# Where three groups of reads are queued in a fused attention gradient kernel: q's first weights, output weights, transposing reads

## The chip, the cores and the metric

The kernel runs on one core of a Trainium2 chip. The metric is the device time of one execution in microseconds; here it is the median of the runs of the kernel before and, after the change, of the changed kernel's runs beside it. A core has five engines that run their own instruction streams in order: PE (matmul, with its weight loads shown apart as PEld), DVE, ACT and POOL (element-wise work), and SP, which here only issues DMAs. POOL and ACT issue DMAs too. All DMAs of the core share 16 DMA engines.

## The reference, cut to what matters

Two attention blocks over 2048 rows of 448 values, 16 heads of 28, forward and gradient, all in bfloat16. Block A is linear attention with the feature map `phi`; block B is softmax attention with one key and value head shared by all 16 query heads.

```
def A(x, wqkv, wo):
    q, k, v = split_heads(x @ wqkv)
    pq, pk = phi(q), phi(k)          # phi(t) = where(t > 0, t + 1, exp(t)) + 1e-6
    kv = einsum("bhsd,bhse->bhde", pk, v);  z = einsum("bhsd->bhd", pk)
    num = einsum("bhqd,bhde->bhqe", pq, kv)
    den = einsum("bhqd,bhd->bhq", pq, z)[..., None] + 1e-6
    return merge_heads(num / den) @ wo

def B(x, wq, wk, wv, wo):
    q = split_heads(x @ wq);  k = x @ wk;  v = x @ wv
    p = softmax(einsum("bhqd,bkd->bhqk", q, k) * 28 ** -0.5)
    return merge_heads(einsum("bhqk,bkd->bhqd", p, v)) @ wo

out, vjp = jax.vjp(lambda *a: concat([A(a[:3]), B(a[3:])], -1), A_x, A_wqkv, A_wo, B_x, B_wq, B_wk, B_wv, B_wo)
return (out, *vjp(grad_out))
```

## The kernel before

Three stages follow each other.

*Prologue (up to the first scores).* `load_xb` reads B's x in four chunks of 512 rows on SyncE; `wq_nat` gets q's weights on POOL's queue, the first four heads (`G0` columns) ahead of the rest, each with one read for 384 rows and one for the last 64; ACT's queue reads k's and v's weights. On PE, `xb_tr(k)` transposes a chunk (ACT evacuates one half at L723, DVE the other at L725). `wq_pads` (L747) copies q's weights into a layout of 32 columns a head; `wkv_pads` (L727 to L734) does that for k and v and replicates them. `q_first` projects the first four heads of chunk 0 and computes the norm of each q row on DVE (L761 to L797); `kv_nat`, `k_sq` and `kv_rep` project k and v, take the norms of k, and write k transposed four times over (`kT_rep`). The largest k norm (`kmax_bc`, L907) and the q norm give an upper bound of each score, which is put in as an extra column (`q_col`), so that the exponential needs no row maximum. Then POOL issues the reads of A's weights (L888, L889), the 16 reads of B's output weights `woB_pr` (L894, one for each head) and those of A's x (L896).

*Forward sweep (256 steps, L1232).* A step takes four heads, 512 query rows and 128 key rows: PE forms scores (`pe_s`, `s_ps`), ACT takes the exponential (`act_e`, L990, two instructions a step), SyncE writes the result to DRAM (`write_e`, L997, 512 KB a step), PE accumulates the output (`pe_o`, `oacc`). The tile `e` comes from a pool of 5 buffers, so a step's exponential waits until the write of five steps ago has landed. Between these, `block` takes pieces off lists by a budget: each piece has a cost, and a step adds `pace(s)` to the budget, 1.15 for the first 128 steps. The order is fixed when the program is built, in the order of the code; a DMA in a piece goes to its engine's queue at that place and waits there for its inputs, with everything behind it.

The first list, `later`, holds the rest of B's q work: `q_rest`, then `bigs` (`q_proj` for chunks 1 to 3, and `kv_rep` for v), each followed by its `smalls[n]`: transposes of q and weights, `pad_next`, and `woT_f`, which transposes the output weights. In `q_proj`, DVE copies the projection (L778), POOL squares it (L779), and two steps later DVE sums it (L782); after the fourth, `q_norm` follows. Then come the pieces of block A (`pieces_A`): projections with `phi`, `G_part`, the rounds `p3_nd` to `p3_dk` over 16 row tiles, which need grad_out transposed (`gaT`), gradients of weights (`gw_all`), and the rounds `p5_dp0` to `p5_gx`, which need x transposed again (`xT`). `chunk_T` (L156 to L159) makes such a transposed chunk of 512 rows and 512 columns with one transposing DMA on SyncE from SBUF to SBUF. `p3_nd(i)` asks for the next chunk of `gaT` at i % 4 == 3; its source `ga` is read by `ga_load` after the round of `gwo` in which the old one was last used. `xT2(0)` stands ahead of `gw_all(3)`, and `p5_dp0(i)` asks for the next chunk at i % 4 == 1. `load_gbT` (L1036) reads and transposes B's part of grad_out from DRAM, 128 columns at a time, and `load_quarter` and `load_e` (L1173, L1165) read back the written exponentials, transposed.

*Backward sweep (L1348) and weight gradients (L1381 on).* Not touched by the change.

Of the kernel before, what the change touches and what calls it, by code (L numbers as in the profile page):

```python
# [12 lines left out]
BF16 = mybir.dt.bfloat16  # L13
# [4 lines left out]
D = 448  # L18
P = 128
# [5 lines left out]
def kernel(  # L25
# [21 lines left out]
    nc = tc.nc  # L47
# [3 lines left out]
    NQC = S // 512  # L51
# [89 lines left out]
    def pieces_A(gen, pl, post, flush, pre_tiles, pk_d, early, swap_pools):  # L141
# [3 lines left out]
        def piece(cost, cap=None):  # L145
            def add(fn):
                out.append((cost, fn, cap))
                return fn
            return add

        V = {}
# [4 lines left out]
        def chunk_T(src, nm):  # L156
            t = chk.tile([P, 4, 4, P], BF16, name=nm, tag="chunk")
            nc.sync.dma_start_transpose(t[:].rearrange("p b c s -> p (b c) s"), src.rearrange("p b d -> p (b d)"))
            return t  # L159

        def xchunk(qc):
            return V["x"][:, qc * 4:(qc + 1) * 4, :]

# [149 lines left out]
            V["gq"] = Halves(halves, "gq_A")  # L313

        def p3_nd(i):
            if i % 4 == 3 and i // 4 < 3:
                V["gaT", i // 4 + 1] = chunk_T(V["ga", i // 4 + 1], "gaT")
            ps = gen([P, 512], "ps_nd")
            for g in range(4):
                mm(ps[:, g * P:(g + 1) * P], V["pq"][:, i, g * P:(g + 1) * P], V["kvz"][:, g, :])  # L320
            rden = awk.tile([P, H, 1], F32, name="rden_A", bufs=3)
            nc.vector.reciprocal(out=rden[:], in_=hv(ps[:, :])[:, :, 0:1])
            nc.vector.tensor_tensor(out=hv(V["onat"][:, i, :]), in0=hv(ps[:, :]),
                                    in1=rden[:].to_broadcast([P, H, 32]), op=ALU.mult)
            V["rden", i] = rden
# [169 lines left out]
        def gw(src, c, q, bi):  # L495
            if q == 0:
                V["acc"] = gen([P, 512], "gw_acc")
            acc = V["acc"]
            for st in range(2 * q, 2 * q + 2):
                mm(acc[:, :], V["x"][:, st, c * P:(c + 1) * P], V[src][:, st, :], start=(st == 0), stop=(st == NS - 1))  # L500
            if q == 7:
                out_gw(acc, c, bi)

        def gw_all(c):
            for q in range(8):
                piece(0.43, 1.3)(lambda c=c, q=q: gw("gq", c, q, 0))
                if q % 4 == 3:
                    piece(0.0)(lambda k=2 * c + q // 4: part_pk2(k))
# [8 lines left out]
            V["natq"] = load_wnat(0, "wqA2")  # L517

        gw_all(0)

        def xT2(qc):
            V["xT", qc] = chunk_T(xchunk(qc), "xaT2")

        def wT_pad(nm):
            nat = V.pop("natq" if nm == "q" else "natk")
# [16 lines left out]
        gw_all(2)  # L542
        for g in range(4):
            piece(0.25)(lambda g=g: wT_tr("k", g))
        piece(0.0)(lambda: xT2(0))
        gw_all(3)

        def p5_dp0(i):
            if i % 4 == 1 and i // 4 < 3:
                xT2(i // 4 + 1)  # L550
            ps = gen([P, 512], "ps_dpk")
            for c in range(2):
                mm(ps[:, :], V["xT", i // 4][:, i % 4, c, :], V["Wp"][:, c, :], start=(c == 0), stop=False)
            V["dpk"] = ps
# [132 lines left out]
    def load_xb(k):  # L687
        nc.sync.dma_start(xb_n[k][:], Bx2[k * 512:(k + 1) * 512, :].rearrange("(b p) d -> p b d", p=P))

    for k in range(NQC):  # L690
        load_xb(k)
    G0 = 4 * DH
    wq_nat = w4.tile([P, 4, D], BF16, name="wqB_nat", tag="w4")
    nc.gpsimd.memset(wq_nat[0:64, 3, :], 0.0)
    for lo, hi in ((0, G0), (G0, D)):
        nc.gpsimd.dma_start(wq_nat[:, 0:3, lo:hi], B_wq[0:384, lo:hi].rearrange("(c p) f -> p c f", p=P))
        nc.gpsimd.dma_start(wq_nat[64:128, 3, lo:hi], B_wq[384:448, lo:hi])
    wkv_nat = tmp.tile([P, 4, 2 * DH], BF16, name="wkv_nat")
    nc.gpsimd.memset(wkv_nat[0:64, 3, :], 0.0)
    for i, w in enumerate((B_wk, B_wv)):  # L700
# [15 lines left out]
    def xb_tr(k):  # L716
        for c2 in range(2):
            tp = gen([P, 1024], "xbT_ps", BF16)
            for c in range(2):
                tr4(tp, lambda b: xb_n[k][:, b, XOFF[2 * c2 + c]:XOFF[2 * c2 + c] + P], 4 * c)  # L720
            dst = xbT[k][:, 2 * c2:2 * c2 + 2, :].rearrange("p c s -> p (c s)")
            if c2 == 0:
                nc.scalar.copy(out=dst, in_=tp[:, :])  # L723
            else:
                nc.vector.tensor_copy(out=dst, in_=tp[:, :])  # L725
# [20 lines left out]
    def wq_pads(h0, h1):  # L746
        nc.vector.tensor_copy(  # L747
            out=wq_pad[:].rearrange("p c (h x) -> p c h x", x=32)[:, :, h0:h1, 1:1 + DH],
            in_=wq_nat[:].rearrange("p c (h e) -> p c h e", e=DH)[:, :, h0:h1])

    def q_first():
        qn_t[0] = ptmp.tile([P, 4, 512], BF16, name="qn", bufs=3)
        nrm_t[0] = ptmp.tile([P, 4, H], F32, name="nrm2")
        pq = gen([P, 4, P], "projN_ps")
        for b in range(4):
            for dc in range(4):
                mm(pq[:, b, :], xbc(dc, b * P, P), wq_pad[:, dc, 0:P], start=(dc == 0), stop=(dc == 3))
        nc.scalar.copy(out=qn_t[0][:, :, 0:P], in_=pq[:, :, :])
        qsq = ptmp.tile([P, H, 32], F32, name="qsq")
        qv = qn_t[0][:].rearrange("p b (h c) -> p b h c", c=32)[:, :, 0:4, :]  # L760
        nc.vector.tensor_tensor(out=qsq[:].rearrange("p (b h) c -> p b h c", b=4), in0=qv, in1=qv, op=ALU.mult)  # L761
        nc.vector.tensor_reduce(out=nrm_t[0][:, :, 0:4], in_=qsq[:].rearrange("p (b h) c -> p b h c", b=4),
                                axis=AX.X, op=ALU.add)
        return upper_sqrt(ptmp, nrm_t[0][:, :, 0:4], [P, 4, 4], 0.5, "root4")
# [97 lines left out]
    def k_sq(hf):  # L862
# [2 lines left out]
        nc.vector.tensor_tensor(out=ksq[:, a], in0=kn[:, a, :], in1=kn[:, a, :], op=ALU.mult)  # L865
        nc.vector.tensor_reduce(out=kn2[:, a], in_=ksq[:, a], axis=AX.X, op=ALU.add)

    wq_pads(0, 4)
    xb_tr(0)
    rootq0 = q_first()  # L870
    wkv_pads()
    xb_tr(1)
    kv_nat(0)
    kv_nat(1)
    xb_tr(2)
    k_sq(0)
    kv_nat(2)
    kv_rep(0, 0, True)
    xb_tr(3)
    kv_nat(3)  # L880
    k_sq(1)
    for hf in range(2):
# [3 lines left out]
    for off in (D, 0, 2 * D):  # L886
# [1 line left out]
        nc.gpsimd.dma_start(nat[:, 0:3, :], A_wqkv[0:384, off:off + D].rearrange("(c p) f -> p c f", p=P))  # L888
        nc.gpsimd.dma_start(nat[0:64, 3, :], A_wqkv[384:448, off:off + D])  # L889
        nats.append(nat)  # L890
    for g in range(4):
        for j in range(4):
            h = 4 * g + j
            nc.gpsimd.dma_start(woB_pr[g][32 * j + 1:32 * j + 1 + DH, :], B_wo[h * DH:(h + 1) * DH, :])  # L894
    for k in range(2):
        nc.gpsimd.dma_start(x_nat.h[k][:, :, 0:D],  # L896
                            Ax2[k * S // 2:(k + 1) * S // 2, :].rearrange("(t p) d -> p t d", p=P))
# [2 lines left out]
    rootk = upper_sqrt(tmp, kcol[:], [P, 1], 0.5, "rootk")  # L900
    kdiag = tmp.tile([P, P], F32, name="kdiag")
    nc.vector.tensor_scalar(out=kdiag[:], in0=identF[:], scalar1=rootk[:, 0:1], scalar2=None, op0=ALU.mult)
    for b in range(1, 4):
        kv_rep(0, b, True)
    kbc_ps = gen([P, P], "kbc_ps")
    nc.tensor.matmul(kbc_ps[:, :], lhsT=onesF[:, :], rhs=kdiag[:, :], start=True, stop=True)
# [22 lines left out]
    for n in range(4):  # L929
        smalls[n + 4].append((0.3, lambda g=n: wqT(g)))  # L930
    smalls[5].append((0.25, wkvT))
    for n in (6, 9, 12):
        smalls[n].append((0.0, pad_next))
    for n, ci in ((7, 0), (10, 1), (14, 2), (15, 3)):
        smalls[n].append((0.25, lambda ci=ci: woT_f(ci)))
    for g in range(4):
        smalls[8 + g // 2].append((0.25, lambda g=g: q_tr(1, g)))
# [544 lines left out]
```

## Time and profile before

| | |
|---|---|
| time, median of 3 runs | 1329.32 us (1326.28 to 1336.55) |
| the profiled execution: time | 1330.31 us |
| the profiled execution: span | 1328.2 us, mean granted clock 0.971 |
| first score on PE | 29.40 us |
| forward sweep (first to last exponential) | 29.9 to 634.7 us |
| backward sweep | 638 to 1273 us |
| busy share of the span: PE, DVE, ACT, POOL | 93%, 71%, 80%, 19% |
| DMA: moved, mean rate | 321.76 MB, 242 GB/s |

Lines of the trace give the start and the length of an instruction or a run of equal ones in us, the engine, the line of the code, the operation, what it writes and reads, and how many; in brackets stands the idle time of the engine just before it and what ended it. SPq is SyncE's queue of DMA issues: the length there is the time of issuing, not of the transfer. Lines of waits give the sum in us, the number and the longest. A granted clock of 0.50 means that PE runs at half speed. The DMA share is the time that packets took, over 16 engines; it can pass 1.

### The profile page before, as it was taken

How to read it: one execution, taken by the hardware profiler on the slowest of the kernel's cores; microseconds unless marked ns; L12 is line 12 of the kernel's file. 1: busy time of each engine (PE TensorE's matmuls, PEld its weight loads, DVE VectorE, ACT ScalarE, POOL GpSimd, SP SyncE). 2: the span in 40 equal slices, each digit the busy share in tenths (PEclk: the TensorE clock that was granted, in tenths of full speed). 3: DMA queues.
4: the chain of work that ended last, by engine and by line, in shares of the span. 5: the costliest groups of instructions: out<-in, count | busy, mean ns of one | idle time of the engine just before them, and what ended most of it. 6: DMA issues, size and time to landing. Idle time of an engine off the chain costs nothing.

```text
span 1328.2 us, 30263 instructions
## 1 busy us (share of the span) xinstructions
PE 1233.2 (93%) x12630; PEld 595.0 (45%) x12690; DVE 940.1 (71%) x1211; ACT 1061.8 (80%) x1176; POOL 250.6 (19%) x317
## 2 busy tenths in 40 slices
PE   6878899888988998998899999999999999999998
PEld 4332234344422333332455555555555555555554
DVE  4775527677743334420789999999999999999942
ACT  3669998778877898996688888888888888888851
POOL 4510032333422112110013111111111111111110
PEclk7889999999989899998899999999999999999999
DMA  3766889589779989889999999999999999999832
GB/s 113 282 211 257 288 324 305 210 309 294 264 287 279 322 299 299 303 287 319 243 238 231 216 230 223 227 214 230 234 219 223 211 218 229 223 223 219 191 124 69
DMA packets 627193, 321.76 MB, mean 242 GB/s; under 512 B 572256, under 2 KB 587600, under 8 KB 626800
## 3 DMA queue, kind: packets, MB, share of 16 engines
q1 hardware_dynamic: 615984, 293.28, 86.6%
q0 software_dynamic: 9088, 26.45, 6.3%
q8 instruction: 99, 1.62, 0.6%
q10 hardware_dynamic: 1984, 0.10, 0.1%
q14 instruction: 38, 0.31, 0.1%
HBM read 23.71 MB, written 153.45 MB: 133 GB/s over the span
## 4 chain that ended last, share of the span: by engine, by line
PE 72%; issue 8%; ACT 7%; DVE 6%; POOL 3%; DMA 3%; SPq 1%; ACTq 0%; POOLq 0%; DVEq 0%
PE dsT_ps L89 19%; PE dp_ps L105 12%; PE akv L108 11%; PE s_ps L105 6%; PE dq_ps L108 5%; ACT e L990 4%; PE oacc L108 3%; DMA edram<-e 3%; PE ps_gx L85 2%; ACT phi_ex L168 2%; PE ps_gxB L85 1%; PE gwq_acc L85 1%; PE G_ps L85 1%; PE gwoB_ps L85 1%; PE ps_go L85 1%
## 5 line engine op out<-in xcount | busy, mean ns | idle before, releaser
L1279 DVE TENSOR_TENSOR ds<-dp_ps,eN 128x1024 bf16<-128x1024 f32 x512 | 604.8, 1220 | 25.5 <-PE dp_ps L105 13.0
L990 ACT ACTIVATE e<-s_ps 128x1024 bf16<-128x1024 f32 x512 | 499.6, 1077 | 105.3 <-issue 33.7
L1301 ACT ACTIVATE dsT<-dsT_ps 128x1024 bf16<-128x1024 bf16 x512 | 496.8, 1023 | 93.3 <-PE dsT_ps L89 93.1
L89 PE MATMUL dsT_ps<-identB,ds 128*128 128x128 bf16 x4096 | 274.8, 220 | 0.0
L89 PEld LDWEIGHTS <-ds 128*128 128x128 bf16 x4096 | 230.5, 98 | 59.3 <-issue 59.2
L105 PE MATMUL s_ps<-qT_B,kT_rep 32*128 32x512 bf16 x1024 | 185.5, 392 | 36.4 <-ACT e L990 30.2
L1331 POOL TENSOR_TENSOR dkv<-dkv,asb 128x512 f32<-128x512 f32 x60 | 76.1, 1268 | 494.1 <-ACT asb L1330 489.0
L108 PE MATMUL akv<-ds,qn_b 128*32 128x512 bf16 x1024 | 156.7, 386 | 0.0
L105 PE MATMUL dp_ps<-vT_rep,doT_b 32*128 32x512 bf16 x768 | 150.0, 387 | 3.5 <-DVE ds L1279 2.4
L105 PEld LDWEIGHTS <-kT_rep 32*128 32x128 bf16 x1024 | 53.6, 91 | 199.3 <-issue 190.6
L108 PE MATMUL akv<-eN,don_b 128*32 128x512 bf16 x768 | 117.7, 387 | 0.0
L108 PE MATMUL dq_ps<-dsT,kn 128*32 128x512 bf16 x1024 | 105.4, 379 | 0.2 <-ACT dsT L1301 0.2
L108 PE MATMUL oacc<-e,vaug 128*32 128x512 bf16 x1024 | 80.9, 393 | 0.0
L105 PEld LDWEIGHTS <-doT_b 32*128 32x128 bf16 x768 | 36.2, 91 | 95.8 <-issue 72.8
L108 PEld LDWEIGHTS <-kn 128*32 128x32 bf16 x1024 | 33.1, 97 | 39.9 <-issue 8.0
L105 PE MATMUL dp_ps<-vT_rep,doT_q 32*128 32x512 bf16 x256 | 49.6, 384 | 0.0
L596 DVE CAST gx_sb<-ps_gx 128x448 bf16<-128x448 f32 x16 | 10.0, 624 | 48.9 <-PE ps_gx L85 48.9
L108 PEld LDWEIGHTS <-don_b 128*32 128x32 bf16 x768 | 21.9, 94 | 43.9 <-issue 43.9
L169 DVE TENSOR_SCALAR phi_ex<-phi_ex 128x512 f32<-128x512 f32 x32 | 14.8, 462 | 34.2 <-ACT phi_ex L168 34.0
L108 PE MATMUL akv<-eN,don_q 128*32 128x512 bf16 x256 | 38.9, 384 | 0.0
L1330 ACT ACTIVATE asb<-akv 128x512 f32<-128x512 f32 x60 | 36.3, 605 | 0.0
L349 POOL TENSOR_SCALAR dph_A<-oq_A 128x512 bf16<-128x512 bf16 x16 | 30.6, 1912 | 29.9 <-issue 27.7
(286 smaller groups left out, 1226.5 us busy)
## 6 DMA issues: line engine op xcount, KB each, us to landing
edram<-e SPq DMA_DIRECT2D x256, 512.0 KB
eN<-edram SPq DMA_TRANSPOSE x137
pk_d<-pkn_A POOLq DMA_DIRECT2D x2, 1024.0 KB, 5.4
onat_d<-onat_q POOLq DMA_DIRECT2D x4, 512.0 KB, 6.3
pk_A<-pk_d POOLq DMA_DIRECT2D x8, 256.0 KB, 8.2
qn_b<-qn_d SPq DMA_DIRECT2D x16, 128.0 KB
on_nat<-onat_d SPq DMA_DIRECT2D x4, 512.0 KB
xb_nat<-in_B_x_dram SPq DMA_DIRECT2D x4, 448.0 KB
```

What stands on the lines that cost most here:

```text
L85: nc.tensor.matmul(out_ap, lhsT=lhsT, rhs=rhs, start=start, stop=stop, tile_position=(0, 0))
L89: nc.tensor.transpose(out_ps_ap, in_ap, ident[0:k, 0:k], tile_position=(0, 0))
L105: nc.tensor.matmul(out_ap, lhsT=lhsT, rhs=rhs, start=True, stop=True, tile_position=(32 * j, 0))
L108: nc.tensor.matmul(out_ap, lhsT=lhsT, rhs=rhs, start=start, stop=stop, tile_position=(0, 32 * c))
L168: nc.scalar.activation(out=ex[:], in_=ps[:, :], func=ACT.Exp)
L169: nc.vector.tensor_scalar(out=ex[:], in0=ex[:], scalar1=1.0, scalar2=1e-6, op0=ALU.min, op1=ALU.add)
L349: nc.gpsimd.tensor_scalar(out=dph[:], in0=oq[:, 512:1024], scalar1=-1e-6, scalar2=1.0, op0=ALU.add, op1=ALU.min)
L990: nc.scalar.activation(out=es[s][:].rearrange("p a j q -> p j a q")[:, 2 * hf:2 * hf + 2], in_=sps.pop(h)[:].rearrange("p j (a q) -> p j a ...
L1279: nc.vector.tensor_tensor(out=ds[:], in0=dps.pop(h)[:], in1=eNs[i][:, 2 * hf:2 * hf + 2, :], op=ALU.mult)
L1301: nc.scalar.activation(out=dsTs[kcu][:].rearrange("p t j q -> p j t q")[:, 2 * hf:2 * hf + 2, :, b * P:(b + 1) * P], in_=tps.pop(h)[:], fu ...
L1330: nc.scalar.activation(out=asb[:], in_=akv[:, :], func=ACT.Copy)
L1331: nc.gpsimd.tensor_tensor(out=dkv[:, kc * 512:(kc + 1) * 512], in0=dkv[:, kc * 512:(kc + 1) * 512], in1=asb[:], op=ALU.add)
```

## The change

q's first-group weights are read on SyncE behind chunk 0 of x and ahead of chunks 1 to 3; the second group stays on POOL. The copies `wq_pads` and `wkv_pads` stand behind the first evacuation, chunk 1's transposes go ahead of `q_first`, and the norm part of `q_first` becomes `q_first_norm`, behind `kv_nat(1)`. `kv_rep(0, 0)` joins the other three. The reads of `woB_pr` leave the end of the prologue for the slots 2 to 5 of the pieces, four in each, and the first `woT_f` moves from slot 7 to 8. `gaT` is made in two halves (at i % 4 == 2 and 3), and the later `xT` in four parts of 128 rows: those of chunk 0 among the pieces of `gw_all(3)`, those of the next chunk one in each round. In the built program SyncE issues 15 more transposes and 2 more reads.

```diff
+        def part_T(key, src, b0, b1):
+            if b0 == 0:
+                V[key] = chk.tile([P, 4, 4, P], BF16, name=key[0] + "_c", tag="chunk")
+            nc.sync.dma_start_transpose(V[key][:, b0:b1].rearrange("p b c s -> p (b c) s"),
+                                        src[:, b0:b1].rearrange("p b d -> p (b d)"))
...
         def p3_nd(i):
-            if i % 4 == 3 and i // 4 < 3:
-                V["gaT", i // 4 + 1] = chunk_T(V["ga", i // 4 + 1], "gaT")
+            if i % 4 >= 2 and i // 4 < 3:
+                b0 = 2 * (i % 4 - 2)
+                part_T(("gaT", i // 4 + 1), V["ga", i // 4 + 1], b0, b0 + 2)
...
+        def xT2(qc, b):
+            part_T(("xT", qc), xchunk(qc), b, b + 1)
+
         def gw_all(c):
             for q in range(8):
+                if c == 3 and q % 2 == 0:
+                    piece(0.0)(lambda b=q // 2: xT2(0, b))
...
-        def xT2(qc):
-            V["xT", qc] = chunk_T(xchunk(qc), "xaT2")
...
-        piece(0.0)(lambda: xT2(0))
         gw_all(3)
 
         def p5_dp0(i):
-            if i % 4 == 1 and i // 4 < 3:
-                xT2(i // 4 + 1)
+            if i // 4 < 3:
+                xT2(i // 4 + 1, i % 4)
...
-    for k in range(NQC):
-        load_xb(k)
...
-    for lo, hi in ((0, G0), (G0, D)):
-        nc.gpsimd.dma_start(wq_nat[:, 0:3, lo:hi], B_wq[0:384, lo:hi].rearrange("(c p) f -> p c f", p=P))
-        nc.gpsimd.dma_start(wq_nat[64:128, 3, lo:hi], B_wq[384:448, lo:hi])
+
+    def load_wq(eng, lo, hi):
+        eng.dma_start(wq_nat[:, 0:3, lo:hi], B_wq[0:384, lo:hi].rearrange("(c p) f -> p c f", p=P))
+        eng.dma_start(wq_nat[64:128, 3, lo:hi], B_wq[384:448, lo:hi])
+
+    load_xb(0)
+    load_wq(nc.sync, 0, G0)
+    for k in range(1, NQC):
+        load_xb(k)
+    load_wq(nc.gpsimd, G0, D)
...
+
+    def q_first_norm():
         qsq = ptmp.tile([P, H, 32], F32, name="qsq")
...
+    xb_tr(0)
     wq_pads(0, 4)
-    xb_tr(0)
-    rootq0 = q_first()
     wkv_pads()
     xb_tr(1)
+    q_first()
     kv_nat(0)
+    xb_tr(2)
     kv_nat(1)
-    xb_tr(2)
+    rootq0 = q_first_norm()
+    xb_tr(3)
     k_sq(0)
     kv_nat(2)
-    kv_rep(0, 0, True)
-    xb_tr(3)
     kv_nat(3)
...
-    for g in range(4):
+
+    def load_woB(g):
         for j in range(4):
...
-    for b in range(1, 4):
+    for b in range(4):
         kv_rep(0, b, True)
...
+    for g in range(4):
+        smalls[2 + g].append((0.0, lambda g=g: load_woB(g)))
...
-    for n, ci in ((7, 0), (10, 1), (14, 2), (15, 3)):
+    for n, ci in ((8, 0), (10, 1), (14, 2), (15, 3)):
         smalls[n].append((0.25, lambda ci=ci: woT_f(ci)))
```

## The prediction, made before any run of the changed kernel

> **What bounds the kernel now.** I read the page first, then the time by stage (busy time in stretches of 33 us), then the list of waits, then the order of time around each place that the change touches. Columns of a stretch: its length, busy time (and instructions) of PE, its weight loads, DVE, ACT, POOL, the granted clock, the share of the DMA engines, GB/s.
>
> ```profile
> span 1328.2 us, 30263 instructions
> 0.00:33.00 33.00, 20.81 (x183) 13.44 (x185) 13.39 (x48) 12.48 (x17) 15.23 (x38) 0.79 0.39 111
> 33.00:66.00 33.00, 26.62 (x178) 10.41 (x180) 22.87 (x54) 20.69 (x22) 19.16 (x27) 0.85 0.77 286
> 396.00:429.00 33.00, 28.76 (x205) 10.39 (x207) 10.83 (x26) 27.55 (x30) 7.45 (x14) 1.00 1.06 299
> 759.00:792.00 33.00, 33.00 (x442) 18.16 (x438) 32.06 (x28) 28.39 (x33) 5.07 (x4) 1.00 1.13 218
> ACT e L990 <- DMA edram<-e: 24.3, 15, 7.7
> ```
>
> The backward sweep (759 us stands for it) keeps PE busy for all of its 33 us; the change does not enter it, so I carry it over. In the first 66 us no engine is full and the clock is not at 1.0: waits decide there. Around 400 us the DMA engines are full, and the last row says that ACT, which paces the forward sweep with its exponentials, stood 24.3 us in 15 waits for an `edram<-e` write to free a buffer of `e`. The change can win in those two places only. The profiled execution took 1330.31 us, 2.1 more than its span and 1.0 more than the median of three runs (1329.32); I sum against 1330.31.
>
> **Part 1, up to the first score.** q's first four heads need `wqB_nat`'s first group, read through POOL's queue.
>
> ```profile
> 4.86 1.44 PE L89 MATMUL xbT_ps<-identB,xb_nat 128*128 128x128 bf16 x16
> 9.81 0.29 DVE L747 COPY wqB_pad<-wqB_nat 128x448 bf16<-128x448 bf16 x1 [6.74 <-DMA wqB_nat<-in_B_wq_dram]
> 10.24 2.17 PE L85 MATMUL projN_ps<-wqB_pad,xb_T 128*128 128x128 bf16 x16 [3.94 <-DVE wqB_pad L747]
> 15.92 1.12 PE L85 MATMUL kv_ps<-wkv_pad,xb_T 128*128 128x64 bf16 x18 [1.80 <-DVE wkv_pad L728]
> 27.84 0.29 DVE L907 TENSOR_REDUCE kmax_bc<-kbc_ps 128x1 f32<-128x128 f32 x1 [0.64 <-PE kbc_ps L906]
> 29.40 0.52 PE L105 MATMUL s_ps<-qT_B,kT_rep 32*128 32x512 bf16 x4 [0.52 <-DVE qT_B L814]
> ...
> 6.30:9.50 3.20, 0.00 (x0) 0.00 (x0) 0.00 (x0) 0.60 (x1) 2.32 (x8) 0.93 1.12 303
> 9.50:19.50 10.00, 6.91 (x78) 6.35 (x79) 4.94 (x19) 1.81 (x3) 0.00 (x0) 0.51 0.02 5
> 9.80:27.20 17.40, 12.92 (x143) 9.83 (x144) 10.01 (x34) 6.48 (x10) 1.56 (x4) 0.73 0.00 1
> ```
>
> PE ends the first transposes at 6.30 and stands until 10.24, because DVE's copy of the weights waits for the read to land at 9.81; DVE's own evacuation at L725 is queued behind that copy. Afterwards, from 9.80 to 27.20, PE is busy for 12.92 of 17.40 us: about 4.5 idle, 0.44 of it the end of the first wait and 1.80 the wait for `wkv_pad`. The change puts the read on SyncE behind chunk 0 of x, puts the copy behind the evacuations, and puts `wkv_pads` and chunk 1's transposes ahead of `q_first`, so both waits lose their cause. What is late next: chunk 1 of x, now behind two small reads. At 303 GB/s a 448 KB chunk takes 1.5 us; chunk 0 was there before 4.86, so chunk 1 comes near 6.9 with 0.5 for the weights, and PE restarts at about 7.0. Then 7.0 + 12.92 + the 2.2 us of waits that I leave = 22.1 in place of 27.2: **-5.1 us**. Bounds: only the first wait goes, and only until DVE's evacuation could have been done (6.30 + 0.7), -2.8; no waits left at all, 27.2 - 7.0 - 12.92, -7.3. I take the middle, since the norm on DVE (moved behind the third transposes) and x's chunks 2 and 3, each held on SyncE for one earlier read, keep some of the waits. Everything from `kmax_bc` to the first score (27.84 to 29.40) moves with it unchanged. The chain's four k projections now follow each other just before it; they were all in the 12.92.
>
> The clock fell from 0.93 to 0.51 after that idle stretch, and the 6.91 us of PE work behind it ran at half speed. The Trainium skill (TensorE: Matmul & The Clock Gate, Part 1) says that one idle window of about 3.4 us throttles PE; the 3.94 us wait agrees. By that rule a wait of under 1 us would leave the clock up, and the estimate would be up to 3.4 us lower, near 1311.6; DVE and ACT pace part of that work, so I do not take it.
>
> **Part 2, output weights off POOL's early queue.**
>
> ```profile
> 29.88 8.16 POOL L894 DMA_DIRECT2D woB_pr<-in_B_wo_dram  x16
> 33.98 0.56 DVE L778 CAST qn<-projN_ps 128x384 bf16<-128x384 f32 x1 [4.20 <-PE projN_ps L85]
> 39.58 0.65 PE L105 MATMUL s_ps<-qT_B,kT_rep 32*128 32x512 bf16 x4
> 39.87 3.18 POOL L779 TENSOR_TENSOR qsq<-qn 128x384 f32<-128x384 bf16 x4
> 42.00 0.68 DVE L778 CAST qn<-projN_ps 128x512 bf16<-128x512 f32 x1
> 42.59 1.04 DVE L782 TENSOR_REDUCE nrm<-qsq 128x12 f32<-128x384 f32 x2
> 45.92 0.61 PE L89 MATMUL qT_ps<-identB,qn 128*128 128x128 bf16 x4 [4.72 <-DVE qn L801]
> 43.50:50.50 7.00, 4.58 (x28) 1.55 (x28) 3.87 (x11) 2.05 (x2) 1.79 (x2) 0.53 0.89 351
> 46.50:62.00 15.50, 14.59 (x107) 5.55 (x108) 11.48 (x29) 11.63 (x13) 6.85 (x7) 0.89 0.77 307
> ```
>
> Sixteen issues hold POOL for 8.16 us, so the squares of q, whose input is there at 34.5, start at 39.87; DVE's norm follows and PE stands 4.72 us for it. Without them the squares follow their inputs. DVE then is next: its copy of the next projection, which PE has done before 39.58, can run at 39.6 instead of 42.0, and what follows it, 42.59 to 45.86, keeps its 3.3 us: 39.6 + 0.7 + 3.3 = 43.6, -2.3 us. Half the stall goes, and PE, which ran at 0.53 behind it for 4.58 us of work, may keep its clock; I count 1.0 of the possible 2.3. The price: the same 8.16 us now lie among the pieces, in four groups behind the squares of four consecutive projections. From 46.5 to 62 POOL has 6.85 busy of 15.5, 8.65 free, which is just enough, but the groups come within some 10 us of it. Squares wait behind a group, and behind them DVE's in-order sum; a group is 8.16 / 4 = 2.0 us, one group's delay less the sum's slack of two steps costs 0 to 2.0, all four uncovered 8.2. I take +1.6, near one group. The first output-weight transposes stand one slot later and need the last group landed; no wait counted. Together **-1.7** (-4.6 to +5.9).
>
> **Part 3, transposing reads in parts.**
>
> ```profile
> L158 SPq DMA_TRANSPOSE xaT<-xa_nat x4: 4011/4546/12612, 416.7 to 500.3; - x4
> L1036 SPq DMA_TRANSPOSE gbT_q<-in_grad_out_dram x16: 1248/1514/2605, 134.1 to 622.3; - x16
> 411.92 1.94 ACT L990 ACTIVATE e<-s_ps 128x1024 bf16<-128x1024 f32 x2 [0.88 <-DMA edram<-e]
> 416.74 4.75 SPq L158 DMA_TRANSPOSE xaT<-xa_nat  x1
> 421.58 5.08 SPq L997 DMA_DIRECT2D edram<-e  x5
> 426.84 12.61 SPq L158 DMA_TRANSPOSE xaT<-xa_nat  x1
> 432.80 1.89 PE L85 MATMUL ps_dpk<-Wp_A,xaT 128*128 128x512 bf16 x4 [5.52 <-DMA xaT<-xa_nat]
> 433.99 2.85 ACT L990 ACTIVATE e<-s_ps 128x1024 bf16<-128x1024 f32 x3 [7.69 <-DMA edram<-e]
> 439.50 7.70 ACT L990 ACTIVATE e<-s_ps 128x1024 bf16<-128x1024 f32 x8 [1.25 <-PE s_ps L105]
> 510.90 5.61 ACT L990 ACTIVATE e<-s_ps 128x1024 bf16<-128x1024 f32 x6 [3.25 <-DMA edram<-e]
> 93.00:98.00 5.00, 3.54 (x37) 1.84 (x31) 2.94 (x12) 3.21 (x5) 0.00 (x0) 1.00 1.10 208
> 418.00:434.00 16.00, 9.84 (x60) 3.37 (x61) 3.28 (x10) 7.88 (x10) 1.38 (x3) 0.84 1.16 173
> 433.00:434.00 1.00, 1.00 (x3) 0.30 (x2) 0.00 (x0) 0.01 (x1) 0.00 (x0) 0.50 1.02 417
> ```
>
> A 512 KB chunk moves at 208 GB/s when two transposes have the engines nearly alone (93 to 98: 2.5 us each), but from 418 to 434 the DMA engines, full at 1.16, made only 173 GB/s: chunk 0, issued at 416.74, is awaited by PE until 432.80. The e writes of 421.58 stand behind it, and ACT stands 7.69 us, then 1.25 on a slow clock. In parts of 128 KB, `p5_dp0(0)` needs one part, and e writes pass between parts. If a part goes as slowly as the chunk did (13.5 / 4 = 3.4 us, an e write 512 KB / 417 GB/s = 1.3), the write between parts 0 and 1 lands near 424, the next near 432, the ones behind part 3 near 436. A buffer of `e` comes up again five steps, some 11 us, after its write: they are just in time. I take **-7.5** of 8.9; bounds -8.9 and +4 (the parts and chunk 1's parts make one longer queue). Chunk 3's 3.25 at 510.90 has the same cause; with its parts one per round, **-2.0** (-3.25 to 0). Chunk 2 made no wait of ACT: 0. Twelve more issues cost SP, at gbT's 1.5 us for 128 KB, nothing: four are 6 us against 4.5, on a queue that otherwise issues one write per step.
>
> `gaT` in halves removes no wait of ACT; it moves the first half one round ahead, which is a new wait:
>
> ```profile
> 261.08 0.79 POOL L228 DMA_DIRECT2D ga_chunk<-in_grad_out_dram  x1
> DMA to landing us min/median/max: 6.2/7.2/8.4
> 268.92 3.08 SPq L158 DMA_TRANSPOSE gaT<-ga_chunk  x1
> ```
>
> The built program has three e writes between the halves, so SyncE reaches chunk 2's first half near 261, where its source has just been asked for; it lands near 268.5. Three e writes queue behind the waiting half for up to 7 us, and ACT waits for them only if they land over 11 us after they were due. Chunk 3 is alike. **+1.0** (0 to +5).
>
> **The sum.** -5.1 - 1.7 - 7.5 - 2.0 + 1.0 = -15.3; 1330.31 - 15.3 = **1315.0**. The forward sweep is paced by ACT and PE in program order, so a shift there is kept to the end.
>
> **The rivals.** *The DMA engines, not the order, make the waits.* Against parts speaks the share of 1.06 around 400 us: the same bytes must pass, and a wait that leaves one write turns up at the next. Then part 3 gives 0 and 1330.3 - 5.1 - 1.7 + 1.0 = 1324.5. For it: ACT waited for a write at 411.92 already, before the first of these transposes. Against it: ACT stood idle while its writes were held by one transfer.
>
> *Slower: a part costs nearly what a chunk does.* Place: SyncE's ring from 416 to 514. If each of 16 parts holds the full engines for gbT's longest 2.6 us instead of a quarter of the median chunk, 1.1, that is 16 x 1.5 = 24 us more on a queue without room, and with no gain from part 3: 1324.5 + 24 = 1348.5. It outweighs parts 1 and 2 from 0.4 us per part, and is over 1% slower from 1.2. Against it speak gbT's 16 reads of the same size, with a median of 1.5 of issuing, and 208 GB/s for unbroken transposes. The Trainium skill (DMA: Bandwidth & Descriptors, Anatomy of one DMA) gives about 2.0 us fixed for a DMA issued from GpSimd, mostly the receipt of the last write; were SyncE's 15 additional transposes to pay it one after another, the estimate is 30 us, 1354.5; no row here shows such a queue of them.
>
> *Part 1 does not do what it says*: chunk 1 of x comes so late behind the small reads (10 us or more) that PE stands as before: 1330.3 - 10.2 = 1320.
>
> **How the numbers follow.** Forecast 0.62, its own range 1308 to 1321; DMA-bound 0.20; slower 0.09; chunk 1 late 0.09. The best ends of parts 1, 2 and 3 together would be 1306. The range 1306 to 1328 leaves out the slower rival and little else. What a measurement of this kernel can tell from no change is about 1%: faster is below 1316. The forecast lies on the edge: two thirds of its chance, 0.42, and some 0.04 of the others are below, so faster 0.46; same 0.45; slower 0.09.
>
> **What would show it.** Right: the first score near 24 us, no wait of `wqB_pad` for its DMA, a wait of `qT_ps` near 2.4 instead of 4.72, ACT's wait for `edram<-e` near 14 instead of 24.3 with none over 3, no wait of `ps_dpk` for its transpose. Wrong: ACT's waits for e writes unchanged in sum (first rival), transposing parts of over 2.6 us (second), a wait for `xb_nat` above 3 us (third), or new waits of DVE's sums for POOL near 50 to 60 us, or of ACT near 270.

## The result and the profile after

The changed kernel took 1319.28 us, the median of 12 runs (1308.24 to 1324.30); the kernel before, beside it, 1327.95 (12 runs, 1325.02 to 1336.55). The ratio is 0.9921, 95% interval 0.9896 to 0.9947: 0.8% faster, 4.3 us above the forecast of 1315.0 and inside its range. The execution that was profiled is the shortest of the twelve (1308.24 us, span 1306.5, mean granted clock 0.981), 11 us under the median. What it shows is a good case, and the experiments have to say how much of it is in every execution.

The time by stage of the changed kernel (columns as before):

```profile
0.00:33.00 33.00, 25.29 (x226) 13.67 (x226) 18.36 (x58) 18.77 (x23) 16.82 (x37) 0.95 0.66 207
33.00:66.00 33.00, 26.16 (x187) 10.00 (x188) 27.25 (x63) 20.48 (x23) 19.65 (x29) 0.90 0.65 245
396.00:429.00 33.00, 32.05 (x246) 12.12 (x244) 12.89 (x30) 30.61 (x33) 5.29 (x10) 1.00 1.06 335
759.00:792.00 33.00, 33.00 (x442) 18.11 (x439) 32.30 (x28) 28.22 (x31) 3.80 (x3) 1.00 1.11 227
```

And from its list of waits (sum, number, longest):

```profile
ACT e L1009 <- DMA edram<-e: 14.1, 13, 2.7
```

PE works 32.05 of the 33 us from 396 on, where it had 28.76, and the DMA engines, as full as before (1.06), move 335 GB/s in place of 299. (The stretch is the same in time, not in work: the changed kernel is some 10 us further on there.) ACT's waits for writes fell from 24.3 to 14.1 us, none over 2.7. The backward sweep is as it was. From 33 to 66 us PE is busy no longer than before (26.16 against 26.62, at a clock of 0.90 against 0.85) and DVE is much fuller: one wait there is shorter, and a new one has come.

The prologue in the timeline:

```profile
7.37 0.28 DVE L760 COPY wqB_pad<-wqB_nat 128x448 bf16<-128x448 bf16 x1
7.81 1.07 PE L89 MATMUL xbT_ps<-identB,xb_nat 128*128 128x128 bf16 x16 [1.09 <-DMA xb_nat<-in_B_x_dram]
8.72 1.06 PE L85 MATMUL projN_ps<-wqB_pad,xb_T 128*128 128x128 bf16 x16
...
19.58 0.29 DVE L924 TENSOR_REDUCE kmax_bc<-kbc_ps 128x1 f32<-128x128 f32 x1 [0.64 <-PE kbc_ps L923]
...
21.15 0.40 PE L105 MATMUL s_ps<-qT_B,kT_rep 32*128 32x512 bf16 x4 [0.52 <-DVE qT_B L829]
```

The weights' copy waits no more; PE waits 1.09 us for chunk 1 of x instead, its clock stays up (the same projection takes 1.06 us, 2.17 before), and the first score comes 8.25 us earlier. Further on, in the same timeline:

```profile
34.80 0.40 PE L89 MATMUL qT_ps<-identB,qn 128*128 128x128 bf16 x4 [2.31 <-DVE qn L816]
...
53.37 0.89 PE L89 MATMUL woTps<-identB,woB_pr 128*128 128x128 bf16 x4
...
55.50 0.61 DVE L806 TENSOR_SCALAR root<-nrm 128x64 int32<-128x64 int32 x1
...
57.47 0.37 DVE L816 TENSOR_SCALAR qn<-root,kmax_bc 128x64 bf16<-128x64 f32 x1
57.64 0.44 DVE L860 COPY woT_B<-woTps 128x512 bf16<-128x512 bf16 x1
...
58.13 1.86 PE L85 MATMUL projN_ps<-wqB_pad,xb_T 128*128 128x512 bf16 x4 [2.83 <-DVE woT_B L860]
59.93 0.60 PE L105 MATMUL s_ps<-qT_B,kT_rep 32*128 32x512 bf16 x2
...
60.63 3.99 ACT L1009 ACTIVATE e<-s_ps 128x1024 bf16<-128x1024 f32 x4 [5.38 <-issue]
```

The wait of `qT_ps` for the norm went from 4.72 to 2.31 us, as forecast (2.4). But there is a wait that the kernel before does not have. The output-weight transposes are done at 54.3; their evacuation on DVE (L860) stands behind the chain of a later norm (L806 to L816) and starts at 57.64. PE's products and transposes of this stage take turns in three PSUM tiles (`psGen`, `bufs=3`); behind `woTps` come two transposes of q, so PE's next projection needs the tile of `woTps` again. It waits 2.83 us for it, the scores behind it in PE's order stand too, and ACT has nothing for 5.38 us. In the kernel before, one slot earlier, the same copy stood ahead of the norm's chain (L791 on):

```profile
63.77 1.02 PE L85 MATMUL projN_ps<-wqB_pad,xb_T 128*128 128x512 bf16 x4 [0.68 <-DVE qn L778]
64.60 0.40 DVE L845 COPY woT_B<-woTps 128x512 bf16<-128x512 bf16 x1
...
65.20 3.82 ACT L990 ACTIVATE e<-s_ps 128x1024 bf16<-128x1024 f32 x4 [1.48 <-issue]
...
66.23 0.61 DVE L791 TENSOR_SCALAR root<-nrm 128x64 int32<-128x64 int32 x1
```

Where the shift arises is seen by following one instruction through both traces: the start of the n-th of the 512 exponentials, less its start in the profile of before. The columns are named by the time in the kernel before, the last before the span is an instruction of the backward sweep (DVE's `ds`, L1279 in the kernel before, L1298 in the changed one).

| profile of | 29.9 | 65.2 | 101.5 | 343.4 | 418.2 | 451.5 | 561.1 | 746.0 | span |
|---|---|---|---|---|---|---|---|---|---|
| the changed kernel | -8.4 | -11.9 | -9.7 | -9.9 | -12.7 | -21.0 | -22.4 | -22.1 | 1306.5 |
| the same, second profile | -5.9 | -8.7 | -3.6 | -4.2 | -3.1 | -11.1 | -10.1 | -9.9 | 1318.6 |
| part 1 alone | -5.4 | -5.9 | -8.3 | -8.5 | -10.3 | -10.2 | -11.0 | -11.9 | 1316.2 |
| part 2 alone | +2.0 | +0.8 | +5.3 | +8.5 | +11.0 | +9.5 | +8.7 | +10.6 | 1338.9 |
| x in parts alone | 0.0 | +0.9 | -1.6 | -1.6 | -1.7 | -10.2 | -10.5 | -7.1 | 1321.5 |
| transposes moved alone | +2.0 | +1.3 | +5.2 | +8.5 | +6.8 | +3.9 | +2.3 | +3.9 | 1332.2 |
| part 2 undone | -4.8 | -3.2 | -7.0 | -4.8 | -7.4 | -15.8 | -17.7 | -17.1 | 1311.1 |
| transposes in slot 9 | -6.1 | -9.5 | -5.7 | -5.9 | -8.2 | -16.4 | -15.7 | -15.1 | 1313.4 |

These are single executions; the times below are medians. Part 2 alone and the transposes moved alone start at +2.0, though nothing ahead of that point was changed in them: PE ran at half clock for 17.1 us of their prologue, and for 10.2 us in the profile of before. So some 2 us in any row belong to the execution.

### The profile page after: what moved, and what is told of

The parts are those of the page before. It is cut to its first block, busy times and chain, and to the rows that moved or that the text cites. A ratio compares the mean times of both kernels' runs of the same rounds, so it can differ in the third digit from the quotient of the medians.

```text
span 1306.5 us, 30339 instructions
## 1 busy us (share of the span) xinstructions
PE 1234.5 (94%) x12690; PEld 591.3 (45%) x12690; DVE 941.6 (72%) x1211; ACT 1062.0 (81%) x1176; POOL 249.5 (19%) x315
## 4 chain that ended last, share of the span: by engine, by line
PE 77%; ACT 8%; DVE 6%; DMA 3%; issue 2%; POOL 2%; SPq 2%; ACTq 0%; POOLq 0%; DVEq 0%
PE dsT_ps L89 20%; PE dp_ps L105 13%; PE akv L108 11%; PE s_ps L105 7%; ACT e L1009 5%; PE dq_ps L108 5%; PE oacc L108 4%; PE ps_gx L85 3%; DMA edram<-e 2%; ACT phi_ex L174 2%; PE gw_acc L85 1%; PE ps_gxB L85 1%; PE G_ps L85 1%; PE gwq_acc L85 1%; PE ps_go L85 1%
## 5 line engine op out<-in xcount | busy, mean ns | idle before, releaser
L1298 DVE TENSOR_TENSOR ds<-dp_ps,eN 128x1024 bf16<-128x1024 f32 x512 | 604.5, 1219 | 25.1 <-PE dp_ps L105 12.6
```

The source lines that it names most:

```text
L1298: nc.vector.tensor_tensor(out=ds[:], in0=dps.pop(h)[:], in1=eNs[i][:, 2 * hf:2 * hf + 2, :], op=ALU.mult)
```

## The experiments

**One part at a time, and the change again.** Four kernels beside the same 27 runs of the kernel before (1329.32 us). The first three are the kernel before with the lines of the diff for one part:

```diff
+    load_xb(0)
+    load_wq(nc.sync, 0, G0)
...
+    rootq0 = q_first_norm()
```

> Part 1 alone: q's first-group weights second on SyncE and the reordered prologue; output weights and transposing reads as before. Theory A (each part is worth what the first profile of the changed kernel shows at its place, and the parts add up): the first exponential at 21.6 us instead of 29.95 and the shift kept to the end, a span of 1328.2 - 8.4 = 1320, time near 1321, ratio 0.994. Rival B (the stall at 45.9 us waits for POOL's 16 issues, which do not move with the first score, so part of the shift is lost there): the shift is under 5 us after 60 us, time 1325 or more.

```diff
+        smalls[2 + g].append((0.0, lambda g=g: load_woB(g)))
...
+    for n, ci in ((8, 0), (10, 1), (14, 2), (15, 3)):
```

> Part 2 alone: the 16 output-weight reads in four groups among the pieces, prologue and transposing reads as before. Theory A: the exponentials between 30 and 97 us come 1 to 1.5 us earlier in the end (a gain of 4 near 55 us, most of it given back by a new stall near 60), time -1.3, ratio 0.999. Rival (the gain of 4 at 55 us is kept when the prologue does not move too, because the output-weight transposes then have more time): -4, ratio 0.997. Rival (the squares behind the groups cost more than the stall): +2 to +6.

```diff
+                    piece(0.0)(lambda b=q // 2: xT2(0, b))
...
+                xT2(i // 4 + 1, i % 4)
```

> The four chunks of the transposing read of x in 128 KB parts alone; gaT whole, prologue and output weights as before. Theory A: no wait of the exponentials over 3 us near 434 and 511, a shift of -8 after 440 us and of -11 from 515 us on, time 1317, ratio 0.9915. Rival (DMA-bound: the first profile of the changed kernel was lucky, and the waits return at the next writes in most executions): -3 to 0, ratio 0.998 or more.

The fourth is the changed kernel as it is.

> The changed kernel unaltered, for a second profile: its first profile is of its fastest execution (1308.2), 11 us under its median. Theory A (the three gains are in every execution, and something after them, which moves with the granted clock, gives up to 14 back): the first exponential at 21.6 again and a shift of -20 at 450 us, with the loss later or in a stall of early forward near 60 us that is longer. Rival (one of the three gains is not in every execution): the first exponential near 26 (clock halved in the prologue) or a wait for an edram write of over 4 us near 434.

Measured: part 1 alone 1321.32, ratio 0.9935 (0.9912 to 0.9958); part 2 alone 1334.42, 1.0038 (1.0018 to 1.0058); x in parts alone 1323.03, 0.9953 (0.9932 to 0.9974); all together 1319.97, 0.9931 (0.9907 to 0.9955). As differences of medians -8.0, +5.1 and -6.3 make -9.2, and the whole change makes -9.4: within intervals of some 3 us each the parts add up, and one of them has the wrong sign.

Part 1 alone took the time that was expected, but its profile has the first exponential at 24.57 us, not at 21.6, and gains 2.4 us more between 65 and 101 us. Part 2 alone has the time of the rival that blamed the squares behind the groups; the next experiment tells the two apart. x in parts alone gave half of what was expected. In the second profile of the changed kernel the first exponential comes at 24.03 us and no wait for a write is over 2.8 us: all three gains are there, the first of them smaller, and what is lost is lost behind the longer stall near 60 us (-8.7 at 65.2, -3.6 at 101.5 in the table).

The timeline of part 2 alone shows the same new wait as the changed kernel, without the moved prologue:

```profile
70.61 0.44 DVE L845 COPY woT_B<-woTps 128x512 bf16<-128x512 bf16 x1
...
71.10 1.86 PE L85 MATMUL projN_ps<-wqB_pad,xb_T 128*128 128x512 bf16 x4 [2.83 <-DVE woT_B L845]
...
73.60 1.02 ACT L994 ACTIVATE e<-s_ps 128x1024 bf16<-128x1024 f32 x1 [5.63 <-issue]
```

In the second profile of the changed kernel this stall is 6.45 us in place of 5.38, followed by far more work at half speed (last section).

**Slot or groups?** Part 2 moves the reads and, by one slot, the first transposes. Only the second:

```diff
-    for n, ci in ((7, 0), (10, 1), (14, 2), (15, 3)):
+    for n, ci in ((8, 0), (10, 1), (14, 2), (15, 3)):
```

> The kernel before, with only the first output-weight transposes moved one slot later (from slot 7 to slot 8); the 16 reads stay in POOL's early queue. Theory S (what part 2 costs is the slot: the transposes' evacuation then stands on DVE behind the row-norm chain of seven operations, PE's next projection waits 2.83 us for that PSUM tile, and the scores behind it wait too): a stall of ACT of 5 us or more near 70 us that the kernel before does not have, a shift of +3 to +5 from 77 us on, ratio 1.003 to 1.004. Rival P (the POOL groups cost it: the squares wait behind reads): no such stall, ratio 1.000.

Next, the changed kernel with part 2 taken back (reads on POOL after the prologue, slot 7):

```diff
-        smalls[2 + g].append((0.0, lambda g=g: load_woB(g)))
...
-    for n, ci in ((8, 0), (10, 1), (14, 2), (15, 3)):
+    for n, ci in ((7, 0), (10, 1), (14, 2), (15, 3)):
```

> The changed kernel without part 2: the 16 output-weight reads in POOL's early queue and the transposes in slot 7 as before; prologue and all transposing reads in parts stay. If the parts add up as their medians alone did (-8.0 for the prologue, -6.3 for the parts of x, +5.1 for part 2): about -14, 1315, ratio 0.989. Rival (part 2 costs only where the prologue has not moved, since with it POOL's issues fall into another stretch): as the changed kernel, ratio 0.993 or more. A stall for POOL's issues like the 4.72 us of the kernel before comes back near 40 us in both.

And the changed kernel with the transposes one slot later still:

```diff
-    for n, ci in ((8, 0), (10, 1), (14, 2), (15, 3)):
+    for n, ci in ((9, 0), (10, 1), (14, 2), (15, 3)):
```

> The changed kernel with the first output-weight transposes one slot later still (slot 9 in place of 8), so that their evacuation stands behind the norm chain no longer. Theory S: the 2.83 us wait of the projection for that evacuation and ACT's stall of 5.4 to 6.5 us near 60 us go down to under 2 us, -4, time near 1315.5, ratio 0.9895. Rival P: no change, ratio 0.993. Rival (the next tile in the pool, a transposed q, holds the projection in its place): the stall shrinks by less than 1.5 us, ratio 0.992.

Measured, beside 16 runs of the kernel before (1329.82): the slot alone 1336.25, ratio 1.0053 (1.0021 to 1.0084); part 2 undone 1313.45, 0.9899 (0.9859 to 0.9938); slot 9 1313.88, 0.9899 (0.9866 to 0.9933). The slot alone, with every read where it was, costs as much as part 2 did (6.4 us in the median; 3.9 of it can be followed in the profile, between 65 and 101 us), and its timeline has the stall:

```profile
70.57 0.44 DVE L845 COPY woT_B<-woTps 128x512 bf16<-128x512 bf16 x1
...
71.06 1.86 PE L85 MATMUL projN_ps<-wqB_pad,xb_T 128*128 128x512 bf16 x4 [2.82 <-DVE woT_B L845]
...
73.56 1.02 ACT L990 ACTIVATE e<-s_ps 128x1024 bf16<-128x1024 f32 x1 [5.15 <-issue]
```

So the groups on POOL are not needed for the loss. Undoing part 2 and moving the slot each give back 3 to 4 us by the ratios (0.9899 against 0.9921 and 0.9931, of about 1329), but their intervals overlap with that of the changed kernel: that either is faster than it is not shown. In the timeline with part 2 undone the old stall returns, longer:

```profile
41.39 0.61 PE L89 MATMUL qT_ps<-identB,qn 128*128 128x128 bf16 x4 [5.46 <-DVE qn L816]
...
42.63 1.02 ACT L1005 ACTIVATE e<-s_ps 128x1024 bf16<-128x1024 f32 x1 [5.96 <-issue]
```

In the timeline with slot 9 it stays away (2.4 us), but the new one does not go down to under 2 us, as was expected:

```profile
61.25 1.98 ACT L1009 ACTIVATE e<-s_ps 128x1024 bf16<-128x1024 f32 x2 [3.62 <-issue]
...
65.63 0.58 PE L85 MATMUL projN_ps<-wqB_pad,xb_T 128*128 128x512 bf16 x1 [1.89 <-DVE woT_B L860]
...
68.55 1.02 ACT L1009 ACTIVATE e<-s_ps 128x1024 bf16<-128x1024 f32 x1 [2.79 <-issue]
```

It falls into two: ACT idles for 3.62 us ahead of any transpose of the output weights, and for 2.79 us behind the projection that waits 1.89 us for L860. Together that is no less than 5.38. One slot later is thus no cure in this profile, and what its median gains is not explained by it.

**The halves of gaT.** The changed kernel with gaT whole:

```diff
-            if i % 4 >= 2 and i // 4 < 3:
-                b0 = 2 * (i % 4 - 2)
-                part_T(("gaT", i // 4 + 1), V["ga", i // 4 + 1], b0, b0 + 2)
+            if i % 4 == 3 and i // 4 < 3:
+                V["gaT", i // 4 + 1] = chunk_T(V["ga", i // 4 + 1], "gaT")
```

> The changed kernel with gaT transposed whole, as before; the rest of the change stays. The prediction's term of +1.0 for the halves would make this 1.0 faster, ratio 0.992; the first profile (ACT's waits for writes of 1.03 us near 302 and 1.54 near 310, a shift that stays at -10.3 from 258 to 315 us) says that the halves cost 0 to 0.4: no difference that can be told from the changed kernel, ratio 0.993.

1318.49, ratio 0.9923 (0.9900 to 0.9946): no difference from the changed kernel that these runs can tell.

**Parts without the spread.** The kernel before with x in parts, all four of a chunk issued at the chunk's old place:

```diff
+        for b in range(4):
+            piece(0.0)(lambda b=b: xT2(0, b))
         gw_all(3)
...
+            if i % 4 == 1 and i // 4 < 3:
+                for b in range(4):
+                    xT2(i // 4 + 1, b)
```

> The kernel before, with x's four chunks transposed in 128 KB parts, but all four parts of a chunk issued one behind another at the chunk's old place. Theory O (order: the writes of e must be able to pass between parts): the writes queue behind four parts as behind a chunk, ACT's wait near 434 us stays at 4 to 9 us, ratio 0.999 to 1.000. Rival D (the size: the first consumer needs one part in place of a chunk, and it is PE's wait for the chunk that holds the scores up): the wait for a write falls under 2 us, ratio 0.995 as for the parts spread over the pieces (1323.0 beside 1329.3).

1326.37 beside 1328.77, ratio 0.9978 (0.9964 to 0.9993), about a third to a half of what the spread parts give (0.9953). In its timeline:

```profile
419.08 5.79 SPq L164 DMA_TRANSPOSE xT_c<-xa_nat  x4
424.96 4.10 SPq L1005 DMA_DIRECT2D edram<-e  x5
429.23 8.93 SPq L164 DMA_TRANSPOSE xT_c<-xa_nat  x4
...
429.53 1.03 PE L85 MATMUL ps_dpk<-Wp_A,xT_c 128*128 128x512 bf16 x4
432.46 3.77 ACT L998 ACTIVATE e<-s_ps 128x1024 bf16<-128x1024 f32 x4 [3.75 <-DMA edram<-e]
```

Both expectations hold in half. PE's product `ps_dpk` waits for no transpose any more (5.52 us in the profile of before), which goes with the smaller size; the five writes issued at 424.96 still stand behind four parts, and ACT waits 3.75 us for one of them. With the parts spread that wait is at most 1.0 us.

**Part 1 without its read.** Only the order of the prologue; the weights come through POOL's queue as before:

```diff
+    xb_tr(0)
     wq_pads(0, 4)
-    xb_tr(0)
-    rootq0 = q_first()
     wkv_pads()
     xb_tr(1)
+    q_first()
...
+    rootq0 = q_first_norm()
```

> Part 1 without its read: q's first-group weights are still read through POOL's queue, as before; only the order of the prologue is the changed one (weight copies behind the evacuations, second chunk's transposes ahead of the first projection). If the order does most of part 1: PE stands for the weights no more, because the second chunk's transposes fill the wait; the first exponential comes 4 to 6 us earlier, ratio 0.995. Rival (the read is the term): under 2 us, ratio 0.9985 or more.

1317.93, ratio 0.9943 (0.9912 to 0.9974), the same as the whole of part 1 (0.9935). Its timeline:

```profile
9.51 0.29 DVE L747 COPY wqB_pad<-wqB_nat 128x448 bf16<-128x448 bf16 x1 [2.59 <-DMA wqB_nat<-in_B_wq_dram]
9.86 1.07 PE L85 MATMUL projN_ps<-wqB_pad,xb_T 128*128 128x128 bf16 x16 [2.40 <-DVE wqB_pad L747]
...
22.24 0.40 PE L105 MATMUL s_ps<-qT_B,kT_rep 32*128 32x512 bf16 x4 [0.52 <-DVE qT_B L816]
```

The weights land as late as before (9.51 against 9.81), but chunk 1's transposes fill a part of the wait, and PE stands 2.40 us in place of 3.94. The read on SyncE exchanges a wait of 2.40 us for the weights for one of 0.99 to 2.77 us (over seven profiles with the read) for chunk 1 of x: no gain.

**Two candidates.** The reads of the output weights leave POOL without going among the pieces: on SyncE, right behind x, transposes in slot 7, the rest as in the changed kernel.

```diff
     for g in range(4):
         for j in range(4):
             h = 4 * g + j
-            nc.gpsimd.dma_start(woB_pr[g][32 * j + 1:32 * j + 1 + DH, :], B_wo[h * DH:(h + 1) * DH, :])
+            nc.sync.dma_start(woB_pr[g][32 * j + 1:32 * j + 1 + DH, :], B_wo[h * DH:(h + 1) * DH, :])
```

> A candidate: the changed kernel with the 16 output-weight reads on SyncE's queue behind x's chunks, as soon as the tiles are cleared, in place of POOL's; the first transposes of the output weights back in slot 7. SyncE issues nothing else between x and the first writes of e, and the DMA engines are nearly idle then. Both costs of part 2 go: no stall of qT_ps for the norm behind POOL's issues (5.46 us at 41 us in the kernel with part 2 undone), no projection held by the output weights' evacuation. Time 1313.5 - 4 = 1309.5, ratio 0.986. Rival (the stall near 41 us is DVE's, not POOL's): 1313, ratio 0.9895. Rival (16 issues on SyncE delay x's chunks or the first writes): above 1315.

The other leaves out of that one what earned nothing, q's weights on SyncE and gaT's halves.

```diff
-    load_xb(0)
-    load_wq(nc.sync, 0, G0)
...
+    for k in range(NQC):
+        load_xb(k)
```

> Only the edits that the runs so far credit: the prologue's order (the weights read on POOL, as before), x's chunks in parts spread over the pieces (gaT whole, as before), and the 16 output-weight reads on SyncE behind x, transposes in slot 7. If the read second on SyncE and gaT's halves are worth nothing: the same as the candidate with them, 1309.3, ratio 0.985. If the read is worth something here: 1311 or more. If it costs (chunk 1 of x came 1.0 to 2.8 us late behind it): 1307 or less.

The first took 1309.26, ratio 0.9851 (0.9811 to 0.9892), the second 1310.59 beside 1330.37, 0.9843 (0.9817 to 0.9869). They are alike, and both beat the kernel before and the changed one: their intervals lie below 0.9896, the lower end of the changed kernel's. They overlap with that of part 2 undone (0.9859 to 0.9938), so that the queue of these reads is worth something by itself is read from the timelines and not shown by the times. From the first one's timeline:

```profile
6.38 9.06 SPq L909 DMA_DIRECT2D woB_pr<-in_B_wo_dram  x16
...
36.52 0.40 PE L89 MATMUL qT_ps<-identB,qn 128*128 128x128 bf16 x4 [2.41 <-DVE qn L816]
...
54.11 1.02 PE L85 MATMUL projN_ps<-wqB_pad,xb_T 128*128 128x512 bf16 x4 [0.65 <-DVE qn L793]
...
54.94 0.40 DVE L860 COPY woT_B<-woTps 128x512 bf16<-128x512 bf16 x1
...
55.54 3.82 ACT L1005 ACTIVATE e<-s_ps 128x1024 bf16<-128x1024 f32 x4 [1.48 <-issue]
```

Sixteen issues take SyncE 9.06 us (POOL 8.16), but SyncE has nothing else to do until the first write of `e`. The wait at `qT_ps` is as short as with part 2 (2.41), and no projection waits for L860, since that copy stands ahead of the norm's chain again.

## Why the prediction was right, and where it was not

The forecast sum of -15.3 us came out as about -9, within the range; the chances put 0.46 and 0.45 on the two sides of -1%, and the result lies on the second, at -0.8%. The signs that it named for being right are all in the first profile: the first score even before 24 us, no wait of `wqB_pad` for its read, 2.31 us at `qT_ps`, 14.1 us of ACT's waits for writes, none of `ps_dpk` for a transpose. But the gain is a little under 60% of the forecast, and that the time came out within 4.3 us is in part luck: the sum started from one execution (1330.31) that was 2.4 us above the median of the runs beside it, and the errors of parts 1 and 2 have opposite signs.

**Part 1 (-5.1): right in kind, short in size, and its credit misplaced.** Alone it gave -8.0 in the median. At the first exponential it gave -4.8 to -8.4 in the seven profiles that hold it whole; -5.1 stands near the low end of that, and -8.4 is -5.1 with the up to 3.4 of the clock that the prediction named and did not take. The profile of before was itself a good case: in the five profiles with the old prologue the first exponential comes at 29.9 to 32.0 us, 31.1 on the mean, in the seven with the whole of part 1 at 23.8 on the mean, which makes -7.3. PE restarted at 7.6 to 9.2 us, not 7.0, because chunk 1 came later than its bytes at 303 GB/s made it. That the gain is one of order, not of the read, the forecast did not separate; the order alone holds all of it as far as these runs can tell (0.9943 against 0.9935).

**Part 2 (-1.7): the step that failed is "The first output-weight transposes stand one slot later and need the last group landed; no wait counted."** The wait for the last group is there, but small (PE's weight load waits 0.2 us in the first profile, PE 0.9 in the second). The slot is what costs: +6.4 us in the median by itself, with the evacuation behind the norm's chain in DVE's order and PE's projection 2.8 us behind that, in all five profiles with slot 8. That wait was to be found in the change of order on DVE and PE, not in the row of any transfer. The other steps held: the stall at `qT_ps` fell from 4.72 to 2.31, and the squares behind POOL's groups cost 0.86 us in one wait of a sum, where +1.6 was taken.

**Part 3 (-7.5, -2.0, +1.0): -6.3 in the median.** The terms add to -9.5 for x. The mechanism holds: writes pass between parts, and ACT's wait near 434 us is down to 1.0 us or less in every kernel with the parts spread. It had been 7.69 us in the profile of before; in the four profiles of other kernels with whole chunks it is 4.28, 4.94, 6.28 and 9.15, 6.5 on the mean of the five, so the term was sized on a somewhat unlucky execution. Chunk 3's 3.25 us is mis-sized for the same reason: the same place shows 1.01 and 1.08 us in two of those four and nothing in two. gaT's halves cost nothing that can be measured, not +1.0. The 13.5 us from which the prediction took 3.4 us for a part stand in no row; the first profile has the parts themselves, below.

**The rivals.** The DMA engines were as full as before and yet moved more, so their load alone did not make the waits. A part does not cost what a chunk does:

```profile
L164 SPq DMA_TRANSPOSE xT_c<-xa_nat x16: 1263/2138/3439, 403.9 to 516.3; - x16
```

(nanoseconds of issuing, least, median and most) the median part holds SyncE for 2.1 us against 4.5 for the median chunk. That is 1.0 us more than a quarter of the median chunk, and the longest is over the 2.6 us that the prediction named as a sign of this rival. But the sixteen parts together hold SyncE for 32.0 us and the four chunks, one of which took 12.61, held it for 25.7: 6 us more in place of 24, over more than 100 us of a queue that had room for them. Chunk 1 of x came late, as the third rival had it, but by 1 to 3 us and not by 10.

## What to carry to other kernels

When work is moved by one slot, list on each in-order engine what its follow-up (here the PSUM evacuation) then stands behind, and who needs the tile that it holds: a copy of 0.44 us moved behind a chain of 2.3 us cost more than moving the DMA issues saved. Ask first whether another queue has nothing to do at that time, before splitting reads into groups on one that has. A stall read in one profile is one draw: before it becomes a term, see whether it stands in a second execution too.

## What was not expected: the clock counts windows, and their phase is a matter of the execution

Why do twelve executions of one program spread over 16 us? In each of the fourteen profiles the granted clock is 1.0 or 0.5 and changes only at steps of 3413 ns, counted from a point that differs from execution to execution. Two executions of the changed kernel at the new stall of part 2, cut at these steps (columns as before; the second number is PE's busy time, the third from the end the clock). First profile:

```profile
54.27:57.68 3.41, 0.78 (x8) 0.54 (x9) 3.20 (x10) 0.98 (x2) 1.27 (x2) 1.00 0.61 234
57.68:61.09 3.41, 2.96 (x14) 0.65 (x13) 2.11 (x6) 0.46 (x1) 0.81 (x2) 0.51 0.39 155
61.09:64.51 3.42, 3.18 (x28) 1.44 (x24) 3.22 (x8) 3.31 (x4) 0.82 (x1) 0.99 0.27 107
```

Second profile:

```profile
57.19:60.60 3.41, 1.64 (x12) 0.83 (x12) 3.34 (x8) 1.26 (x2) 2.08 (x2) 1.00 0.76 299
60.60:64.02 3.42, 1.62 (x4) 0.40 (x3) 2.27 (x8) 0.00 (x0) 0.60 (x1) 0.50 0.17 65
64.02:67.43 3.41, 3.41 (x23) 1.22 (x23) 2.93 (x6) 2.05 (x2) 1.04 (x1) 0.50 0.25 98
67.43:70.84 3.41, 3.41 (x18) 1.22 (x19) 2.15 (x5) 1.94 (x2) 0.10 (x1) 0.50 0.43 172
70.84:74.26 3.42, 3.42 (x29) 1.49 (x30) 1.63 (x4) 2.56 (x3) 1.64 (x2) 1.00 0.51 205
```

The same stall lies in one window there and across two here, and is followed by one window at half speed there and three here. Of the five profiles with slot 8, four have three half windows there; the first profile of the changed kernel is the exception. Counted over all fourteen profiles, from the first clock record of each up to 1280 us, by PE's busy share of a window at full clock:

| busy share | windows | next window at half clock |
|---|---|---|
| under 0.55 | 126 | 124 |
| 0.55 to 0.60 | 37 | 22 |
| 0.60 to 0.65 | 49 | 7 |
| over 0.65 | 4722 | 2 |

From half clock, all 71 windows busy for less than 0.8 were followed by another half one, and so were 28 of 164 that were busy for more than 0.95. The first twelve executions of the changed kernel show what goes with it: from 1308.24 us at a mean clock of 0.981 to 1324.30 at 0.968, a line through them gives 0.39 us of time for each us at half clock (taken as 2 x (1 - mean clock) x span; correlation 0.91). So a change that shortens a stall seems to win twice, and unevenly: over their runs the candidates' mean clock is 0.977 to 0.982 and 0.974 to 0.982, that of part 2 alone 0.960 to 0.970.

The Trainium skill (TensorE: Matmul & The Clock Gate, Part 1) has the window, 3413 ns and free-running, and says that the same kernel varies with its phase: the runs agree. It also says that one idle window lowers the clock; here a window that was about half idle did so (124 of 126 under 0.55), and the measurement decides. Even the drop that the prediction read as agreeing, in the profile of before, follows a window (5.65 to 9.07 us) in which PE was busy for 0.19 of the time. It fits with this that the 1.0 to 2.8 us wait of part 1 left the clock up in the first profile (1.06 us for the first projection) and halved it in the second (1.91): the first projection ran at full speed in three of the seven profiles with the read, so the 3.4 us that the forecast left open are had in some executions only. That the half-busy window is the cause, and not only what comes before, is not shown: no run fills one.
